# A cached attention block with a gated MLP on one core: the last head's V split by batch, the last w_down chunks in smaller loads, 50 rows of w_down in a load of 25 rows

## The chip, the core and the metric

The kernel runs on one core of a Trainium2 chip. The metric is the device time in microseconds (us), the median of three runs. Beside it stands one execution that the hardware profiler recorded; all durations below come from it, and they count from the start of its span. The core's engines are called as in the profile: PE multiplies matrices (PEld: its weight loads), DVE and ACT work on vectors, POOL is used for sums and maxima across partitions, SP issues the transfers, and 16 DMA engines carry them out.

## What is computed

Two tokens (batch 2, one position each) go through a decode step of two parallel branches, attention over a cache and a bilinear gated MLP, both on the normalised input, and both are added to it. All numbers are 32-bit.

```python
B, D, Hq, Sk, Dh, F = 2, 512, 32, 8192, 128, 1376
def attention(x, k_cache, v_cache, wq, wo):
    W = min(4096, max(256, Sk // 4))                # 2048 last positions
    q = (x @ wq) as (B, 32 heads, 1, 128)
    s = q . k_cache[:, :, Sk - W:, :] * Dh ** -0.5
    o = softmax(s) @ v_cache[:, :, Sk - W:, :]
    return o as (B, 1, 4096) @ wo
def glu(x, w_gate, w_up, w_down):
    return ((x @ w_gate) * (x @ w_up)) @ w_down
xn = layernorm(x)
out = x + attention(xn, ...) + glu(xn, ...)
```

## The kernel before

Nearly all of the work is reading: K and V of 32 heads (2048 positions, 2 batches) and the weights are some 159 MB. They are laid out in one `stream` in the order in which they are used. Each load takes 128 rows (one for each SBUF partition), so a load is named here by its columns of 4 bytes: K or V of a head has CK = 4096 columns (2 batches x 16 positions x 128), `wq` and `wo` 512 a head, a chunk of 128 rows of `w_down` 512 columns.

`blocks` (L45) lists the loads. A unit is K of a head with `wq` of a later one, or V of a head with its `wo`; three units make a load of 13824 columns. The last loads are smaller: K of head 31 with V of head 28 and two chunks of `w_down` (9728 columns), V of 29 with its `wo` (4608), V of 30 with its `wo` (4608), V of 31 (4096), `wo` of 31 with chunks 4 to 6 (2048), chunks 7 and 8 (1024), chunk 9 (512). The 96 rows of `w_down` beyond the ten chunks (FR) are packed in 384 columns, `wr`, in an early load. `pump` (L143) issues the loads in order on SP as buffers come free: three step buffers of up to 13824 columns; V of 29 and 30 share one (`late`), all that follows another (`last`). Two small loads follow the third one on SP: `x_nat`, x in 16 rows, and `carry`, a 9 x 9 matrix with two ones.

`InOrder` (L83) makes PE, DVE, ACT and SP issue their instructions in exactly the order in which the code calls them.

For a head h: `products` (DVE: K times q), `sums` (DVE), `maxima` (DVE, then POOL across partitions), `weights` (ACT: `nm`, the scaled maximum, then one exponential for each batch into `p`, with its sum), `reciprocals`. For its V: `weigh` (L329) does eight matrix products, four row groups of the PSUM bank for each of two batches; `copy_out` (ACT) takes the bank to `o_sb`; `transpose` (L346) picks the diagonal parts with four products and scales them into `oT` (ACT, two instructions a head); `project_o` multiplies by `wo` into `acc`. The profile counts each 32-bit product as two matrix instructions, so eight products are x16. `keep_busy(n)` (L326) is a product of n columns whose result nobody reads.

The two batches stand RB = 8 rows apart in `acc`, so that M = 9 rows are kept of which two are used. Up to head 27 `acc` is [9, 512]; after that it is folded: `accumulate` writes four groups of 128 columns to four groups of 32 partitions (`acc_g`), with `carry` as the matrix that moves the sum so far.

The end (L478 to L531) is written out by hand. In order on PE: V of 26 and 27 with fillers, V of 28, two chunks of `w_down`, the fold, head 28's projection, `values([H-3])` for head 29 with a filler of 512 columns before and one after the transposition, then V of 30, a filler of 512, its transposition, a filler of 256, its projection. V of 31 is done in two halves of the columns: eight products of 256 columns into one bank, eight into another (`o_ps2`, half of the tile `spare_t`, zeroed by DVE just before), ACT copying each half; then its transposition, chunks 4 to 6, its projection, chunks 7 to 9. DVE adds `x_nat` to `acc_g` and SP writes `o_out`.

Of the kernel before, what the change touches and what calls it, by code (L numbers as in the profile page):

```python
# [8 lines left out]
F32 = mybir.dt.float32  # L9
AF = mybir.ActivationFunctionType  # L10
# [6 lines left out]
P = 128  # L17
# [9 lines left out]
LAG = 3  # L27
RB = 8
M = RB * (B - 1) + 1
OUT = P  # L30

CARRY = 72
HG = 4
# [5 lines left out]
STEP = 3 * UNIT  # L39
WD = [(0, 2), (2, 4), (4, 7), (7, NFC - 1), (NFC - 1, NFC)]  # L40
NS = 3
FX = FR // NS


def blocks():  # L45

    def wd(n):
        return [("wd", i, D) for i in range(*WD[n])]

    def k(h):
# [15 lines left out]
    loads += [gu(1) + units[0] + units[1] + wd(0) + [("wr", 0, NS * P)]]  # L73
# [40 lines left out]
def kernel(  # L114
    ctx: ExitStack,
    tc: tile.TileContext,
    x_rows: bass.AP,
    carry_rows: bass.AP,
    stream: bass.AP,
# [86 lines left out]

    oT_ring = [const.tile([P, M], F32, name=f"oT{i}") for i in range(4)]
    for t in oT_ring:
        nc.gpsimd.memset(t, 0.0)

# [117 lines left out]

    def weigh(h, v, parts, first, last):  # L329


        for n, part in enumerate(parts):
            b, i = divmod(part, JG)
            pe.matmul(
                o_ps[bank][32 * i : 32 * i + 8 * B, :], p_t[h][:, b, i, :],
                v[:, FB * n : FB * (n + 1)], start=first and b == 0, stop=last and b == B - 1,
            )
# [8 lines left out]
    def transpose(heads, o_sb):  # L346
# [8 lines left out]
        for h in heads:  # L355
            rec = rec_t.pop(h)
            oT[h] = oT_ring[h % 4]
            for b in range(B):
                c = B * side(h) + b
                act.activation(  # L360
                    oT[h][:, RB * b : RB * b + 1], d[:, c : c + 1], AF.Copy,
                    scale=rec[:, b : b + 1],
                )
# [25 lines left out]

    hT = const.tile([P, 4, NFB, M], F32, name="hT")  # L390
    dve.memset(hT, 0.0)

    hX = const.tile([P, NS, M], F32, name="hX")
    dve.memset(hX, 0.0)
# [15 lines left out]
    def gate():  # L410
# [4 lines left out]
        for i in range(4):  # L415
            t = tr[:, P + i * P // 2 : P + i * P // 2 + NFB * B]
            pe.matmul(t, h_sb[:, i * P : (i + 1) * P], rows, start=True, stop=True)
            act.copy(hT[:, i, :, ::RB], t.rearrange("p (n b) -> p n b", b=B))
        for i in range(NS):
            t = tr[:, P + (2 * i + 1) * P // 4 : P + (2 * i + 1) * P // 4 + NFB * B]  # L420
            f = (NFC % 4) * P + i * FX - FR
            pe.matmul(t, h_sb[:, f : f + P], rows, start=True, stop=True)
            act.copy(hX[FR:, i, ::RB], t[FR:, (NFB - 1) * B :])

    def down(n):
        for c in range(*WD[n]):
# [5 lines left out]
            else:  # L432
                accumulate(hT[:, c % 4, c // 4, :], got["wd", c][0], last=(c == NFC - 1))
            done("wd", c)

    def down_rest():
        wr = got["wr", 0][0]
        pe.matmul(
            acc[:, : NS * P], hT[:FR, NFC % 4, NFC // 4, :], wr[:FR], start=False, stop=False
        )  # L440
        for i in range(NS):
# [92 lines left out]
def laid_out(x):  # L534
# [6 lines left out]
    }  # L541
    carry = np.zeros((M, M), a.dtype)
    first["x"][:] = a.reshape(B, P, NC).transpose(1, 0, 2).reshape(P, B * NC)
    for b in range(B):
# [3 lines left out]
        for n in range(NFB):  # L548
            first["rows"][32 * n + b, n * B + b] = 1.0
        carry[RB * b, RB * b] = 1.0  # L550
    cache = {
# [9 lines left out]
    wd = x["B_w_down"]  # L561
    rest = wd[NFC * P :].reshape(FR, NS + 1, P)

    def field(kind, i):
# [10 lines left out]
        if kind == "wr":  # L575
            last = rest[:, NS, :].reshape(NS, FX, P).swapaxes(0, 1)
            return np.concatenate([rest[:, :NS, :], last]).reshape(P, NS * P)
        if kind == "wd":
# [6 lines left out]
    ]  # L585
    x_rows = np.zeros((D // P, 32 // RB, P), a.dtype)
    x_rows[:, :B] = a.reshape(B, D // P, P).transpose(1, 0, 2)
    return {
        "x_rows": x_rows.reshape(-1, P),
        "carry": carry,  # L590
        "stream": np.concatenate(parts),
# [33 lines left out]
```

## Time and profile before

| what | value |
|---|---|
| device time, median of 3 runs | 377.32 us (377.29 to 377.32) |
| span of the profiled execution, first to last instruction | 375.7 us |
| device time less span | 1.6 us |
| moved by DMA | 159.70 MB, mean 425 GB/s |
| PE busy / DVE busy / ACT busy | 256.5 / 294.6 / 58.7 us |
| mean granted PE clock | 0.795 of full |

The page shows one execution. Busy time says little where stages have different limits: the chain of waits, followed back from the last instruction, and the timeline of the end tell more. In a timeline a line is a group of like instructions of one engine: start, time from the first one's start to the last one's end, engine, line of code, operation, output <- input, sizes, count, and in brackets the idle time before it with what ended it. Nearly all lines say L98, the line in `InOrder` that records every call, so groups are told apart by the names of their tiles. The granted clock of PE is given for windows of time.

### The profile page before, as it was taken

The page shows a single profiled execution, that of the slowest core. Times are in us where ns is not written, and L with a number is a line of the kernel's source. Part 1 is how long each engine was busy: PE and PEld are TensorE (multiplying, and loading weights), DVE is VectorE, ACT ScalarE, POOL GpSimd, SP SyncE. Part 2 cuts the span into 40 slices and gives each one's busy share as a digit, 9 for nine tenths or more (in the row PEclk, how much of TensorE's full clock was granted, in tenths as well). Part 3 has the DMA queues.
Part 4 walks back from the last instruction along what each step waited for, and adds up shares of the span by engine and source line. Part 5 has one row for each costly group of instructions (what it writes and reads, how often), then busy time and mean ns, then how long its engine had stood idle before and what let it go on. Part 6 is the DMA issues. An engine that isn't in the chain of part 4 may idle for free.

```text
span 375.7 us, 2891 instructions
## 1 busy us (share of the span) xinstructions
PE 256.5 (68%) x1100; PEld 88.1 (23%) x1100; DVE 294.6 (78%) x147; ACT 58.7 (16%) x259; POOL 25.3 (7%) x78
## 2 busy tenths in 40 slices
PE   3396696986548487864848676485867639637996
PEld 3241122331112122211222211121212213021334
DVE  3299691998599499769949976994996799599960
ACT  1021001122020211201112020111202011121131
POOL 1001000000000000100000100000000000000010
PEclk9796988899696966859686786976669887556999
DMA  8999999899999999999999999999999999999995
GB/s 327 463 436 454 408 426 471 383 465 432 414 465 394 459 424 424 461 400 453 418 437 449 412 447 424 432 442 430 436 436 424 437 434 436 436 425 424 419 421 226
DMA packets 4382, 159.70 MB, mean 425 GB/s; under 512 B 514, under 2 KB 658, under 8 KB 1042
## 3 DMA queue, kind: packets, MB, share of 16 engines
q1 hardware_dynamic: 4370, 159.54, 98.5%
q8 instruction: 8, 0.13, 0.1%
q14 instruction: 4, 0.03, 0.0%
HBM read 159.47 MB, written 0.07 MB: 425 GB/s over the span
## 4 chain that ended last, share of the span: by engine, by line
DMA 62%; DVE 29%; PE 7%; ACT 1%; issue 0%; SPq 0%; DVEq 0%
DMA step<-in_stream_dram 62%; DVE s L98 14%; DVE step L98 14%; PE o_ps L98 3%; PE q L98 2%; PE acc L98 2%; PE tr L98 1%; DVE m L98 0%; ACT o_sb L98 0%; ACT oT L98 0%; SPq L98 0%; DVE rec L98 0%; DVE o_out L98 0%; DVEq L98 0%
## 5 line engine op out<-in xcount | busy, mean ns | idle before, releaser
L98 DVE TENSOR_TENSOR step<-step,q 128x4096 f32<-128x4096 f32 x31 | 136.6, 4408 | 53.3 <-DMA step<-in_stream_dram 53.3
L98 PE MATMUL q<-step,xnb 128*128 128x512 f32 (+1 forms) x128 | 92.7, 874 | 75.5 <-DMA step<-in_stream_dram 75.5
L98 DVE TENSOR_REDUCE s<-step 128x32 f32<-128x4096 f32 x32 | 141.4, 4419 | 1.1
L98 PE MATMUL o_ps<-step,p 128*16 128x512 f32 (+1 forms) x512 | 69.7, 682 | 10.3 <-DMA step<-in_stream_dram 10.3
L98 PEld LDWEIGHTS q<-step,xnb 128*128 128x128 f32 x128 | 32.2, 275 | 128.9 <-DMA step<-in_stream_dram 79.1
L98 PE MATMUL acc<-step,oT 128*9 128x512 f32 (+1 forms) x88 | 35.2, 554 | 9.3 <-ACT oT L98 8.1
L98 PE MATMUL tr<-first,o_sb 128*128 128x2 f32 (+2 forms) x198 | 27.6, 258 | 15.3 <-ACT o_sb L98 12.8
L98 ACT COPY o_sb<-o_ps 128x512 f32<-128x512 f32 (+1 forms) x24 | 13.8, 576 | 143.1 <-PE o_ps L98 143.1
L98 PEld LDWEIGHTS tr<-first,o_sb 128*128 128x128 f32 x198 | 25.5, 196 | 37.3 <-ACT o_sb L98 32.6
L295 POOL PARTITION_ALL_REDUCE mm<-m x32 | 11.3, 354 | 283.4 <-DVE rec L98 178.9
L98 PEld LDWEIGHTS o_ps<-step,p 128*16 128x16 f32 x512 | 13.5, 106 | 70.4 <-issue 55.2
L98 ACT ACTIVATE nm<-mm 128x2 f32<-128x2 f32 x32 | 6.5, 203 | 129.5 <-POOL mm L295 129.5
L98 ACT ACTIVATE p<-s,nm 128x16 f32<-128x16 f32 x64 | 19.2, 300 | 1.0
L98 ACT ACTIVATE oT<-tr,rec 128x1 f32<-128x1 f32 x64 | 12.2, 260 | 28.3 <-PE tr L98 28.3
L311 POOL PARTITION_ALL_REDUCE sum<-rs x32 | 12.7, 398 | 54.8 <-ACT p L98 54.8
L98 PE MATMUL o_ps<-step,xn 128*2 128x512 f32 (+1 forms) x48 | 12.9, 593 | 0.0
L98 ACT ACTIVATION_READ_ACCUMULATOR p<-s,nm 128x1 f32 x64 | 12.0, 187 | 0.0
L98 DVE TENSOR_TENSOR step<-step,tr 128x4096 f32<-128x4096 f32 x1 | 4.4, 4421 | 9.3 <-DMA step<-in_stream_dram 9.3
L98 PEld LDWEIGHTS acc<-step,oT 128*9 128x9 f32 x88 | 4.3, 91 | 19.5 <-ACT oT L98 13.1
L98 PE MATMUL q<-xnb,mean_w 128*128 128x512 f32 (+1 forms) x18 | 8.5, 563 | 0.0
L98 PE MATMUL acc<-step,hT 128*9 128x128 f32 (+2 forms) x58 | 7.9, 357 | 0.0
L98 DVE TENSOR_REDUCE m<-s 128x2 f32<-128x32 f32 x32 | 5.9, 186 | 1.1
(43 smaller groups left out, 36.5 us busy)
## 6 DMA issues: line engine op xcount, KB each, us to landing
step<-in_stream_dram SPq DMA_DIRECT2D x16, 6912.0 KB, 33.7
step<-in_stream_dram SPq DMA_DIRECT2D x2, 6400.0 KB, 32.6
step<-in_stream_dram SPq DMA_DIRECT2D x1, 6720.0 KB, 45.6
step<-in_stream_dram SPq DMA_DIRECT2D x1, 6656.0 KB, 28.9
step<-in_stream_dram SPq DMA_DIRECT2D x1, 5376.0 KB, 15.4
step<-in_stream_dram SPq DMA_DIRECT2D x1, 4864.0 KB, 30.1
step<-in_stream_dram SPq DMA_DIRECT2D x2, 2304.0 KB, 17.2
step<-in_stream_dram SPq DMA_DIRECT2D x1, 2048.0 KB, 15.9
```

Source lines behind the costliest of these rows:

```text
L98: made = call(*args, **kwargs)
L295: nc.gpsimd.partition_all_reduce(mm, m, P, bass_isa.ReduceOp.max)
L311: nc.gpsimd.partition_all_reduce(sum_t[h], rs, P, bass_isa.ReduceOp.add)
```

## The change

- *V of head 31 by batch.* V of 31 is cut by batch into `vh` 0 and `vh` 1, 2048 columns each. `vh` 0 is appended to the load of V of 29 (4608 becomes 6656 columns); `vh` 1 is a load of its own (2048 in place of 4096). PE does batch 0 (`last_half(0)`, four products of 512 columns) after head 29's projection and ahead of V of 30, and batch 1 after head 30's transposition, where the filler of 256 columns was. Both go to `o_ps2`, which DVE now zeroes ahead of head 30's `products`. ACT copies one half of the columns, DVE the other.
- *The last chunks in smaller loads.* Chunks 8 and 9 are cut into halves of 256 columns (64 of each 128). The loads after `wo` of 31 have 768, 512 and 256 columns in place of 1024 and 512. With the 2048 columns ahead of them these are rows of 8, 3, 2 and 1 KB. The products on the halves have 64 columns (`down_half`).
- *The 96 rows beyond the chunks.* 46 of them go, with x itself, into `wr` (256 columns in place of 384); the other 50 into `wd_tail` by a load of its own, 25 rows of 4 KB, in the place of `x_nat` and `carry`, which go. x is now added by the product with `wr`, whose left side gets ones from `rows`; so the last DVE step is a copy. `gate` has two products and four ACT copies for `wr`, and two of each for `wd_tail`, in place of three and three.
- *M = 2.* The batches stand next to each other; `oT`, `hT`, `hX` shrink, their zeroing goes (but `hX`), and `wd_tail` is zeroed on 32 partitions. Two unused tiles (`pad0`, `pad1`) take up space.

```diff
-RB = 8
-M = RB * (B - 1) + 1
+M = B
-WD = [(0, 2), (2, 4), (4, 7), (7, NFC - 1), (NFC - 1, NFC)]
-NS = 3
-FX = FR // NS
+WD = [(0, 2), (2, 4), (4, 7), (7, 8)]
+HD = D // 2
+HP = P // 2
+NT, FT, FP = 2, 25, 28
+FX = FR - NT * FT
+RX = M + FX
+PADS = 96, 248
...
-    out += [(late, v(H - 3)), (late, v(H - 2)), (last, [("v", H - 1, CK)])]
-    out += [(last, [("wo", H - 1, CO)] + wd(2))]
-    return out + [(last, wd(n)) for n in range(3, len(WD))]
+    out += [(late, v(H - 3) + [("vh", 0, CK // B)]), (late, v(H - 2))]
+    out += [(last, [("vh", 1, CK // B)]), (last, [("wo", H - 1, CO)] + wd(2))]
+    halves = [("wh", (c, n), HD) for c in range(WD[-1][1], NFC) for n in range(2)]
+    out += [(last, wd(3) + halves[:1])]
+    return out + [(last, halves[i : i + 2]) for i in range(1, len(halves), 2)]
...
+    const.tile([P, PADS[0]], F32, name="pad0")
+    wd_tail = const.tile([P, NT * D], F32, name="wd_tail")
+    dve.memset(wd_tail[:32, :], 0.0)
...
-    x_nat = const.tile([P, P], F32, name="x_nat")
-    dve.memset(x_nat, 0.0)
-    sp.dma_start(x_nat[::RB, :], x_rows)
-    carry = const.tile([P, CARRY], F32, name="carry")[:M, :M]
-    sp.dma_start(carry, carry_rows)
+    sp.dma_start(wd_tail[FP : FP + FT, :], tail)
+    carry = rows[:M, :M]
...
+    def down_half(c, n):
+        w = got["wh", (c, n)][0]
+        for g in range(4):
+            pe.matmul(
+                acc_g[32 * g : 32 * g + M, n * HP : (n + 1) * HP], hT[:, c % 4, c // 4, :],
+                w[:, g * HP : (g + 1) * HP], start=False, stop=(c, n) == (NFC - 1, 1),
+            )
+        done("wh", (c, n))
...
     def down_rest():
         wr = got["wr", 0][0]
-        pe.matmul(
-            acc[:, : NS * P], hT[:FR, NFC % 4, NFC // 4, :], wr[:FR], start=False, stop=False
-        )
-        for i in range(NS):
+        for i in range(2):
             pe.matmul(
-                acc[:, NS * P :], hX[FR:, i, :], wr[FR:, i * P : (i + 1) * P],
+                acc[:, HD * i : HD * i + HD], hX[: HP + RX, i, :], wr[: HP + RX],
+                start=False, stop=False,
+            )
+        for i in range(NT):
+            pe.matmul(
+                acc, hX[: FP + FT, 2 + i, :], wd_tail[: FP + FT, i * D : (i + 1) * D],
                 start=False, stop=False,
             )
...
     spare, o_ps2 = spare_t[:, 0, :], spare_t[:, 1, :]
+    dve.memset(o_ps2, 0.0)
     products(h)
...
     reciprocals(h + 1)
-    dve.memset(o_ps2, 0.0)
+    def last_half(b):
+        weigh(H - 1, got["vh", b][0], range(b * JG, (b + 1) * JG), b == 0, b == B - 1, o_ps2)
+        done("vh", b)
+    last_half(0)
     o_sb = pv([H - 2])
     keep_busy(GC)
     transpose([H - 2], o_sb)
-    keep_busy(256)
+    last_half(1)
     project_o(H - 2)
     o_sb = small.tile([P, 4 * DH], F32, name="o_sb", bufs=2)
-    v = got["v", H - 1][0].rearrange("p (n k w) -> p n k w", k=2, w=2 * DH)
-    for k, t in enumerate((o_ps[bank], o_ps2)):
-        for n in range(CK // FB):
-            b, i = divmod(n, JG)
-            pe.matmul(
-                t[32 * i : 32 * i + 8 * B, 0 : 2 * DH], p_t[H - 1][:, b, i, :], v[:, n, k, :],
-                start=(b == 0), stop=(b == B - 1),
-            )
-        act.copy(o_sb[:, 2 * k * DH : 2 * (k + 1) * DH], t[:, 0 : 2 * DH])
-    done("v", H - 1)
+    act.copy(o_sb[:, : 2 * DH], o_ps2[:, : 2 * DH])
+    dve.tensor_copy(o_sb[:, 2 * DH :], o_ps2[:, 2 * DH :])
     bank = 1 - bank
     transpose([H - 1], o_sb)
     down(2)
     project_o(H - 1)
     down(3)
-    down(4)
     o_out = const.tile([P, P], F32, name="o_out")
-    dve.tensor_tensor(o_out, acc_g, x_nat, op=ALU.add)
+    const.tile([P, PADS[1]], F32, name="pad1")
+    for c in range(WD[-1][1], NFC):
+        for n in range(2):
+            down_half(c, n)
+    dve.tensor_copy(o_out, acc_g)
```

More of the change, by code (lines that the diff above doesn't have):

```diff
@@ L116 @@
     tc: tile.TileContext,
-    x_rows: bass.AP,
-    carry_rows: bass.AP,
+    tail: bass.AP,
     stream: bass.AP,
@@ L327, in keep_busy, with weigh @@
         pe.matmul(spare[:, 0:n], mean_w, spare_in[:, 0:n], start=True, stop=True)
-    def weigh(h, v, parts, first, last):
+    def weigh(h, v, parts, first, last, into=None):
+        into = o_ps[bank] if into is None else into
         for n, part in enumerate(parts):
@@ L334, in weigh @@
             pe.matmul(
-                o_ps[bank][32 * i : 32 * i + 8 * B, :], p_t[h][:, b, i, :],
+                into[32 * i : 32 * i + 8 * B, :], p_t[h][:, b, i, :],
                 v[:, FB * n : FB * (n + 1)], start=first and b == 0, stop=last and b == B - 1,
@@ L390 @@
     hT = const.tile([P, 4, NFB, M], F32, name="hT")
-    dve.memset(hT, 0.0)
-    hX = const.tile([P, NS, M], F32, name="hX")
+    hX = const.tile([P, 2 + NT, M], F32, name="hX")
     dve.memset(hX, 0.0)
@@ L417, in gate @@
             pe.matmul(t, h_sb[:, i * P : (i + 1) * P], rows, start=True, stop=True)
-            act.copy(hT[:, i, :, ::RB], t.rearrange("p (n b) -> p n b", b=B))
-        for i in range(NS):
[L420 to L423, printed above, removed]
+            act.copy(hT[:, i, :, :], t.rearrange("p (n b) -> p n b", b=B))
+        f = (NFC % 4) * P
+        own = slice((NFB - 1) * B, NFB * B)
+        for i in range(2):
+            t = tr[HP * i : HP * i + RX, P + P // 4 : P + P // 4 + NFB * B]
+            pe.matmul(t, h_sb[:, f - M : f + FX], rows, start=True, stop=True)
+            act.copy(hX[HP * i : HP * i + RX, i, :], t[:, own])
+            one = rows[HP * i : HP * i + M, 2 * i * B : 2 * i * B + B]
+            act.copy(hX[HP * i : HP * i + M, i, :], one)
+        for i in range(NT):
+            t = tr[: FP + FT, P + (2 * i + 3) * P // 4 : P + (2 * i + 3) * P // 4 + NFB * B]
+            f0 = f + FX + i * FT
+            pe.matmul(t, h_sb[:, f0 - FP : f0 + FT], rows, start=True, stop=True)
+            act.copy(hX[: FP + FT, 2 + i, :], t[:, own])
     def down(n):
@@ L561, in laid_out @@
     wd = x["B_w_down"]
-    rest = wd[NFC * P :].reshape(FR, NS + 1, P)
+    rest = wd[NFC * P :]
+    mixed = np.zeros((2, HP, HD), a.dtype)
+    mixed[:, :RX] = np.concatenate([a, rest[:FX]]).reshape(RX, 2, HD).swapaxes(0, 1)
     def field(kind, i):
@@ L575, in field @@
         if kind == "wr":
-            last = rest[:, NS, :].reshape(NS, FX, P).swapaxes(0, 1)
-            return np.concatenate([rest[:, :NS, :], last]).reshape(P, NS * P)
+            return mixed.reshape(P, HD)
+        if kind == "vh":
+            return cache["v"][H - 1][:, i]
+        if kind == "wh":
+            c, n = i
+            return wd[c * P : (c + 1) * P].reshape(P, 4, 2, HP)[:, :, n].reshape(P, HD)
         if kind == "wd":
@@ L585, in laid_out @@
     ]
-    x_rows = np.zeros((D // P, 32 // RB, P), a.dtype)
-    x_rows[:, :B] = a.reshape(B, D // P, P).transpose(1, 0, 2)
     return {
-        "x_rows": x_rows.reshape(-1, P),
-        "carry": carry,
+        "tail": rest[FX:].reshape(NT, FT, D).swapaxes(0, 1).reshape(FT, NT * D),
         "stream": np.concatenate(parts),
@@ L623 @@
     y = r.results[0]["out_0_dram"]
-    return y[[32 * g + RB * b for b in range(B) for g in range(D // P)]].reshape(B, 1, D)
+    return y[[32 * g + b for b in range(B) for g in range(D // P)]].reshape(B, 1, D)
```

14 lines of the change are left out of this document (5 added, 9 removed).

## The prediction

> **What bounds the kernel now.** I read the page first (share of the span, slices, chain of waits), then the chain in order of time, then the timeline of the last 20 us, then the granted clock by 3.41 us windows.
>
> ```profile
> span 375.7 us, 2891 instructions
> DMA  8999999899999999999999999999999999999995
> q1 hardware_dynamic: 4370, 159.54, 98.5%
> DMA 62%; DVE 29%; PE 7%; ACT 1%; issue 0%; SPq 0%; DVEq 0%
> ```
>
> The transfers are full in every slice: 98.5% of 16 engines' span, from the second microsecond to the end. Nothing in the middle of the kernel can be won or lost but by bytes; the chain calls 29% DVE because DVE's work on K is what frees a buffer for the next load. What the change can move is the tail, so that is where the rest of the reading goes.
>
> ```profile
> 352.22 15.87 DMA step<-in_stream_dram
> 368.13 1.06 PE o_ps L98 x16
> ...
> 373.02 0.29 DVE o_out L98
> ```
>
> After the last big wait (V of head 31, used from 368.13) PE has 4.9 us of work up to 373.02. Was PE or the transfer last? This timeline answers (start, duration, engine, group, and in brackets what ended the idle time before it):
>
> ```profile
> 352.41 0.13 PEld L98 LDWEIGHTS o_ps<-step,p 128*16 128x16 f32 x8 [0.78 <-DMA step<-in_stream_dram]
> 357.86 0.41 PE L98 MATMUL acc<-step,oT 128*9 128x128 f32 x8
> 358.08 1.90 PE L98 MATMUL o_ps<-step,p 128*16 128x512 f32 x16
> 360.88 0.95 PE L98 MATMUL tr<-first,o_sb 128*128 128x2 f32 x8
> 361.69 1.10 PE L98 MATMUL q<-xnb,mean_w 128*128 128x512 f32 x2
> 361.86 0.41 ACT L98 ACTIVATE oT<-tr,rec 128x1 f32<-128x1 f32 x2 [1.23 <-PE tr L98]
> 362.57 0.20 ACT L98 ACTIVATE nm<-mm 128x2 f32<-128x2 f32 x1 [0.30 <-POOL mm L295]
> 363.31 0.19 ACT L98 ACTIVATION_READ_ACCUMULATOR p<-s,nm 128x1 f32 x1
> 363.30 1.91 PE L98 MATMUL o_ps<-step,p 128*16 128x512 f32 x16 [0.17 <-DMA step<-in_stream_dram]
> 365.14 1.12 PE L98 MATMUL q<-xnb,mean_w 128*128 128x512 f32 x2
> 366.92 0.68 PE L98 MATMUL q<-xnb,mean_w 128*128 128x256 f32 x2
> 369.98 1.08 PEld L98 LDWEIGHTS tr<-first,o_sb 128*128 128x128 f32 x8 [0.42 <-ACT o_sb L98]
> 370.12 0.37 ACT L98 COPY o_sb<-q 128x256 f32<-128x256 f32 x1 [0.49 <-PE q L98]
> 371.08 0.84 PE L98 MATMUL acc<-step,hT 128*9 128x128 f32 x24
> 371.74 0.40 PE L98 MATMUL acc<-step,oT 128*9 128x128 f32 x8
> 371.96 0.99 PE L98 MATMUL acc<-step,hT 128*9 128x128 f32 x24
> 372.55 0.12 PEld L98 LDWEIGHTS acc<-step,hT 128*9 128x9 f32 x8 [0.25 <-DMA step<-in_stream_dram]
> ```
>
> The last chunk of w_down made PE wait 0.25 us (372.55), V of head 30 0.17 us (363.30), and V of head 29 not at all: PE was still on head 28's projection (357.86 + 0.41) when its multiplication began at 358.08. So in the tail PE and the stream run level, and PE has some 0.4 us to spare in 15. That is the fact on which the forecast turns: the tail has room for no later start of PE.
>
> **The change, part by part.** Every load has 128 rows, so I count columns of the stream. From the first use of the load that carries V of 28 (352.41) to that of V of 30 (363.30) lie 2 x 4608 columns: 9216 / 10.89 = 846 columns a us. V of 29 landed by that at 352.41 + 4608 / 846 = 357.86.
>
> *Half of V31 rides with V29.* The load of 4608 columns becomes one of 6656, and a load is usable only when all of it is there: 352.41 + 6656 / 846 = 360.28, so 2.42 us later. V of 30 is pushed likewise, to 352.41 + 11264 / 846 = 365.73. The second half of V31 lands where all of it did (13312 columns: 368.15), and the w_down loads end where they ended, since 16896 columns remain 16896. What is won: 0.9 us of PE's work on V31 can be done ahead. What it costs: the stretch from V29 on starts 2.20 us later (360.28 against 358.08), and PE works in program order, so everything of heads 29 to 31 stands behind it.
>
> From there by the old rows. Head 29's oT is done at 361.86 + 0.41 = 362.27, now 364.47. ACT runs in order too: head 31's scaled maximum and exponentials stand behind oT of 29 and took from 362.57 to 363.50, now about 364.51 to 365.44. The new first half of V31 needs these, so it can't start at the end of head 29's projection but at 365.44. Eight multiplications of a head take 363.30 to 365.14 = 1.84 us, so four take 0.9: done at 366.34. V of 30 has been waiting since 365.73; its multiplication starts at 366.34, against 363.30 before: 3.04 us late.
>
> From that start on, old distances: up to the small filler after the transposition 366.92 - 363.30 = 3.62 us. There the filler (0.68 us) gives way to the second half of V31, 0.9, makes 4.5. Then the two copies: ACT's half 0.37 as before, the other half on DVE beside it; DVE's own row for such a copy is the 0.67 us below for 512 columns, so about 0.4 for 256; with hand-overs of about 0.2 that is 5.1. Transposition 369.98 to 371.08 less the 0.1 that it waited for the second copy: 6.1. Down-projection of chunks 4 to 6, 371.08 to 371.74: 6.8. Head 31's projection to 371.96: 7.0. Chunk 7, a third of 0.66: 7.2.
>
> ```profile
> 356.80 0.67 DVE L98 COPY acc_sb<-acc 9x512 f32<-9x512 f32 x1
> 325.11 3.61 PE L98 MATMUL o_ps<-step,p 128*16 128x512 f32 x16 [2.83 <-DMA step<-in_stream_dram]
> ```
>
> Chunks 8 and 9 come in halves: 32 matrix instructions of 64 columns for 16 of 128. No row has 64 columns. If the columns set the price it is the old 0.44 us; if the instruction does, 0.88. The nearest row (0.84 for 24 of 128) doesn't tell them apart, so I take the middle, 0.7: 7.9, and 0.2 until DVE sees the result: 8.1. Output copy at 366.34 + 8.1 = 374.44, against 373.02: **+1.4 us**. The bounds on this part: 64 columns 0.26 less or 0.18 more, the exponentials waited for in part only (0.3 less): +0.9 to +1.7.
>
> *Cover that is gone: the clock.* Between head 28's projection (ends 358.27) and V29 at 360.28 PE now has 2.0 us of nothing, with no filler in it. This is what such a gap did elsewhere in this trace (columns: window, its length, PE busy, PEld, DVE, ACT, POOL, granted clock, DMA share, GB/s):
>
> ```profile
> 54.60:58.01 3.41, 2.16 (x10) 0.77 (x8) 2.72 (x4) 0.17 (x1) 0.36 (x1) 1.00 1.16 503
> 58.01:61.43 3.42, 2.16 (x16) 1.70 (x20) 0.00 (x0) 0.81 (x5) 0.00 (x0) 1.00 1.16 501
> 88.73:92.15 3.42, 2.33 (x9) 0.67 (x8) 3.42 (x1) 0.72 (x4) 0.00 (x0) 1.00 1.17 501
> 92.15:95.56 3.41, 0.00 (x0) 0.00 (x0) 0.30 (x3) 0.89 (x5) 0.75 (x2) 1.00 0.71 308
> 136.52:139.93 3.41, 2.19 (x17) 1.07 (x10) 3.38 (x4) 1.00 (x3) 0.13 (x1) 1.00 1.09 470
> 139.93:143.34 3.41, 3.41 (x5) 1.18 (x4) 3.41 (x1) 0.90 (x5) 0.62 (x2) 0.50 1.16 503
> 317.42:320.84 3.42, 2.20 (x15) 1.25 (x12) 3.42 (x1) 1.30 (x5) 0.00 (x0) 1.00 0.93 404
> 320.84:324.25 3.41, 1.44 (x2) 0.00 (x0) 0.28 (x3) 0.89 (x5) 0.75 (x2) 0.50 1.09 472
> 358.38:361.80 3.42, 3.42 (x27) 1.64 (x20) 3.42 (x1) 0.58 (x1) 0.40 (x1) 1.00 0.99 427
> ```
>
> The clock changes only at edges of such windows. After one with PE busy 2.19 or 2.20 us of 3.41 the next ran at 0.50; after 2.33 it stayed at 1.00, and once (54.60) after 2.16. In the tail of before all windows are full and granted 1.00 (last row). With 2.0 us idle a window keeps 1.4 us of work, well under 2.2; only if the edge cuts the gap nearly in half (each part under 1.2 us, some 0.4 us of the 3.4 us of possible positions) does the clock stay. At 0.50 the multiplication of a head takes 3.61 us in place of 1.90 (325.11 above), so a window of 3.41 us does 1.7 us of work and the chain, which is all PE's there, gets **+1.7 us**. Bounds: 0 (clock kept) and 3.4 (two windows). The fillers make this worse: they run for nothing at half rate in front of the transposition.
>
> [...]
>
> *Bytes and the 25-row load.* 13440 columns become 13312 (-64 KB), x's 8 KB and the carry go, 100 KB come: +28 KB, at the mean 425 GB/s +0.07 us. Bounds: 100 KB in 25 rows of 4 KB need not spread evenly. If five engines carry five rows each, these get 20 KB less 4.5, at 425 / 16 GB/s each +0.6 us, and all others -0.17. Every landing is as late as its slowest engine, so -0.2 to +0.6 on all of the tail; I take +0.1.
>
> [...] No row of this trace shows which engine a row took.
>
> *Edits that cost nothing.*
>
> ```profile
> 325.15 4.42 DVE L98 TENSOR_TENSOR step<-step,q 128x4096 f32<-128x4096 f32 x1 [4.00 <-DMA step<-in_stream_dram]
> 364.37 0.48 DVE L98 MEMSET q<- 128x512 f32 x1
> x_nat<-in_x_rows_dram SPq DMA_DIRECT2D x1, 8.0 KB, 45.3
> ```
>
> The memset of the second bank moves from 364.37 to DVE's wait for head 30's K, 4.00 us idle in this trace; without that cover 0.5. The zeroing for the tail rows is 1024 columns wide, about 0.9 us by the row of 512, at a time when DVE waits for its first load. M = 2 for 9 rows changes the weight loads by nanoseconds. Three more ACT copies in the gate and four projections for four others lie early in the kernel, where a load takes far longer than the work on it. The x addition leaves the last DVE step: a copy for the 0.29 at 373.02, at most 0.02 less.
>
> Sum: 1.4 + 1.7 + 0.1 - 0.0 = +3.2. The profiled execution: span 375.7, so 378.9; what lies outside the span (377.32 - 375.7 = 1.6) stays. **Predicted 380.5 us.**
>
> **The rivals.** *Late, but at full clock*: the gap is cut by an edge, or the clock takes a longer gap to fall. Then +1.5: 378.8. For it: the pair 88.73 / 92.15 with 1.1 us idle and the pair 54.60 / 58.01 with 1.25, that did nothing; against it: 2.0 is longer than both. *The end of the stream decides*: PE makes up its delay, and the last landing sets the end as at 372.55. Then 64 columns after it save 0.1, the output copy 0.02, fewer bytes on the lagging engines 0.2: 377.0, not slower. It needs PE to go from V30 to the end in 372.9 - 365.8 = 7.1 us and to be free at 365.8; the rows give 8.1 and 366.3, so fillers or copies would have to cost 1.5 us less than now. *The small load lands on the engines that are last already*: +0.6 on top of the forecast, 381.1.
>
> **How the numbers follow.** Forecast 0.52, full clock 0.27, stream decides 0.15, small load on top 0.06. I leave out the third case and a little beside: 378.0 to 381.3; the forecast's own range is 379.9 to 381.1. About 0.2% (0.75 us) is what a measurement of this kernel can tell from no change. The third case is mostly within that, seldom beyond: faster 0.05, same 0.11, slower 0.84.
>
> **What would show it.** In the profile of the changed kernel: PE idle about 2 us before head 29's multiplication, ended by a transfer; granted 0.50 in one window after it, else 1.00 (full clock); head 30's multiplication with no wait for its V; no wait of PE for the last w_down halves, and the last DVE step near 376. If PE still waits for the last halves, the third case is right and the forecast's main step wrong. If head 29's V is used before 360, the column count is wrong.

## The result and the profile after

The changed kernel takes 378.50 us (median of 7 runs, 378.15 to 380.38), the kernel before 377.27 us in the same rounds (377.01 to 377.32). The ratio is 1.0046, with a 95% interval of 1.0030 to 1.0062: slower, by half a per cent. (It counts all runs, so it lies above the ratio of the two medians, 1.0033.) The seven runs do not scatter about their median: four lie at 378.15 to 378.50 and three at 379.59 to 380.38. The profiled execution is one of the latter (379.59), so it shows a loss that the median run does not have; both losses are taken apart below.

The page of the changed kernel, the rows that answer to those shown of before (span, DMA share by slices, share of queue 1, chain by engine):

```profile
span 377.8 us, 2886 instructions
DMA  8999999999999999999999999999999999999993
q1 hardware_dynamic: 4494, 159.57, 97.9%
DMA 62%; PE 18%; DVE 17%; ACT 2%; issue 1%; SPq 0%; DVEq 0%
```

The stream is as full as before, except in the last slice, 3 tenths in place of 5: the kernel now runs on longer after its transfers are done. Before, the chain of waits had 7% PE; now it has 18%. The chain in order of time (start, duration, what) shows which part that is:

```profile
342.91 17.00 DMA step<-in_stream_dram
...
359.95 1.91 PE o_ps L102 x16
...
365.00 0.86 PE q L102 x8
365.86 1.72 PE o_ps L102 x16
...
370.47 0.38 ACT o_sb L102
...
371.96 3.11 PE acc L102 x72
...
375.09 0.29 DVE o_out L102
```

The last transfer in this chain is V of 29 with its passenger, in at 359.91. From there to the output copy at 375.09 it is PE without a break, but for one copy by ACT. Before, the last transfer in the chain was V of 31, used from 368.13. The timeline of that stretch follows (start, length, engine, group, and in brackets the idle time before it with what ended it). The profile calls the bank of V of 31, `o_ps2`, by the name of its tile, `q`, and so it calls the fillers' bank.

```profile
358.08 0.40 PE L102 MATMUL acc<-step,oT 128*2 128x128 f32 x8
359.95 1.91 PE L102 MATMUL o_ps<-step,p 128*16 128x512 f32 x16 [1.47 <-DMA step<-in_stream_dram]
364.28 0.31 ACT L102 ACTIVATE p<-s,nm 128x16 f32<-128x16 f32 x1
364.59 0.29 ACT L102 ACTIVATE p<-s,nm 128x16 f32<-128x16 f32 x1
364.82 1.04 PE L102 MATMUL q<-step,p 128*16 128x512 f32 x8
365.40 0.11 PEld L102 LDWEIGHTS o_ps<-step,p 128*16 128x16 f32 x4 [0.46 <-DMA step<-in_stream_dram]
365.68 1.90 PE L102 MATMUL o_ps<-step,p 128*16 128x512 f32 x16
370.47 0.37 ACT L102 COPY o_sb<-q 128x256 f32<-128x256 f32 x1 [0.60 <-PE q L102]
370.87 0.42 DVE L102 COPY o_sb<-q 128x256 f32<-128x256 f32 x1 [5.14 <-ACT o_sb L102]
371.89 1.45 PE L102 MATMUL acc<-step,hT 128*2 128x128 f32 x24
373.52 1.53 PE L102 MATMUL acc<-step,hT 128*2 128x128 f32 x40
```

PE waits 1.47 us for V of 29, and V of 30's product starts at 365.68 in place of 363.30, 2.38 us late. Its first weight load waited for V of 30 too (365.40), but the product itself had no idle time before it: it came right behind the first half of V31 (364.82 and the 0.86 us of the chain). Before the last w_down halves PE waits for nothing any more. And the 24 matrix instructions on chunks 4 to 6, which took 0.84 us before, take 1.45. The windows say why (columns: window, its length, busy PE, PEld, DVE, ACT, POOL, granted clock, DMA share, GB/s):

```profile
358.30:361.71 3.41, 1.94 (x24) 0.37 (x16) 3.41 (x1) 0.00 (x0) 0.34 (x1) 1.00 1.02 438
361.71:365.12 3.41, 3.41 (x28) 1.88 (x28) 0.57 (x3) 1.78 (x8) 0.36 (x1) 1.00 0.94 402
368.54:371.95 3.41, 3.14 (x37) 2.17 (x39) 0.42 (x1) 0.79 (x3) 0.00 (x0) 1.00 0.80 309
371.95:375.36 3.41, 3.10 (x73) 2.37 (x72) 0.27 (x1) 0.41 (x2) 0.00 (x0) 0.50 0.00 0
```

The clock did drop to 0.50, but not behind the gap before V of 29, where it was forecast: that window holds 1.94 us of busy PE, and the next was granted 1.00. It dropped behind a window with 3.14 us of busy PE. Both readings contradict the rule of 2.2 us of busy PE that the prediction took from the profile of before.

### The profile page after: what moved, and what is told of

It is laid out like the page before. It is cut to its first block, busy times and chain, and to the rows that moved or that the text cites. A ratio compares the mean times of both kernels' runs of the same rounds, so it can differ in the third digit from the quotient of the medians.

```text
span 377.8 us, 2886 instructions
## 1 busy us (share of the span) xinstructions
PE 256.1 (68%) x1100; PEld 86.9 (23%) x1100; DVE 295.4 (78%) x147; ACT 58.8 (16%) x261; POOL 25.3 (7%) x74
## 4 chain that ended last, share of the span: by engine, by line
DMA 62%; PE 18%; DVE 17%; ACT 2%; issue 1%; SPq 0%; DVEq 0%
DMA step<-in_stream_dram 62%; DVE step L102 8%; DVE s L102 8%; PE o_ps L102 6%; PE q L102 5%; PE acc L102 5%; PE tr L102 3%; ACT o_sb L102 1%; ACT oT L102 1%; SPq L102 0%; ACT hT L102 0%; DVE o_sb L102 0%; DVE m L102 0%; ACT hX L102 0%; DVE o_out L102 0%
## 5 line engine op out<-in xcount | busy, mean ns | idle before, releaser
L102 PE MATMUL o_ps<-step,p 128*16 128x512 f32 x496 | 68.8, 693 | 13.2 <-DMA step<-in_stream_dram 13.2
L102 PEld LDWEIGHTS q<-step,xnb 128*128 128x128 f32 x128 | 32.1, 273 | 128.0 <-DMA step<-in_stream_dram 77.5
L102 PE MATMUL acc<-step,oT 128*2 128x512 f32 (+1 forms) x88 | 33.9, 548 | 9.1 <-ACT oT L102 9.1
L102 PE MATMUL tr<-first,o_sb 128*128 128x2 f32 (+4 forms) x200 | 26.5, 251 | 15.9 <-ACT o_sb L102 13.1
L102 ACT COPY o_sb<-o_ps 128x512 f32<-128x512 f32 x23 | 13.5, 586 | 146.7 <-PE o_ps L102 146.7
L102 PEld LDWEIGHTS tr<-first,o_sb 128*128 128x128 f32 (+2 forms) x200 | 24.4, 188 | 37.5 <-ACT o_sb L102 32.5
L102 PEld LDWEIGHTS acc<-step,oT 128*2 128x2 f32 x88 | 4.0, 88 | 19.7 <-ACT oT L102 14.6
L102 PE MATMUL acc<-step,hT 128*2 128x128 f32 (+2 forms) x72 | 8.2, 411 | 0.0
L102 DVE RECIPROCAL rec<-sum 128x2 f32<-128x2 f32 x32 | 5.0, 155 | 3.3 <-POOL sum L312 3.3
```

The costliest lines, as they stand in the source:

```text
L102: made = call(*args, **kwargs)
```

## The experiments

Each kernel was compared with runs of the kernel before on the same chip, whose medians lie between 377.29 and 377.35 us.

### One half of the change alone, and the other

First the split of V31 in the kernel before (`v_only`), then all of the change but the split (`rest_only`).

```diff
 # v_only, against the kernel before
-    out += [(late, v(H - 3)), (late, v(H - 2)), (last, [("v", H - 1, CK)])]
+    out += [(late, v(H - 3) + [("vh", 0, CK // B)]), (late, v(H - 2))]
+    out += [(last, [("vh", 1, CK // B)])]
...
 # rest_only, against the changed kernel
-    out += [(late, v(H - 3) + [("vh", 0, CK // B)]), (late, v(H - 2))]
-    out += [(last, [("vh", 1, CK // B)]), (last, [("wo", H - 1, CO)] + wd(2))]
+    out += [(late, v(H - 3)), (late, v(H - 2)), (last, [("v", H - 1, CK)])]
+    out += [(last, [("wo", H - 1, CO)] + wd(2))]
```

> The kernel before with the split of V31 alone (first half with V29, second half after V30, both by batch). Theory A: the whole loss is here, 378.1 to 378.6 us in most runs and up to 380.5 in some, PE idle before head 29's product by 1.5 us or more, no wait of PE for the last w_down load. Rival C: about 377.3, no difference.

Measured: 378.49 us (378.25 to 380.06, 5 runs), ratio 1.0036 (1.0023 to 1.0049). The whole loss is there with the split alone.

> All of the change but the split of V31 (V31 again one load behind V30, cut by columns). Theory A (PE starts heads 29 to 31 late because the first half of V31 is loaded with V29): without it the kernel is not slower than before, and the shorter last products and the 25-row load show: 376.8 to 377.1 us, the last w_down landing about 0.3 us earlier than the 372.5 of before. Rival C (the 25-row load or the small last loads hold the stream up): 378 us or more here too.

Measured: 378.01 us (377.14 to 379.81, 12 runs), ratio 1.0018 (1.0007 to 1.0029): far from theory A, and just inside the range that rival C named. The cause that C gives is not seen, though. C has the stream held up, which would lengthen the span. The spans of these runs are 375.3 to 376.9 us with a median of 375.6, against 375.5 for the kernel before; but device time less span, which is 1.7 to 1.9 us in the runs of all the other kernels here, is 1.77 to 3.03 here. So most of the excess of the median lies outside the span, where no engine's instruction is recorded; three of the twelve spans are also longer, 376.3 to 376.9. What either is stays open. The value of the rest of the change is therefore read from another pair, below.

### The load that V of 29 shares

`half_behind30` is the changed kernel with both halves of V31 loaded behind V of 30. `own_load` leaves the first half where it is, but as a load of its own, so that V of 29 need not wait for it.

```diff
 # half_behind30, against the changed kernel
-    out += [(late, v(H - 3) + [("vh", 0, CK // B)]), (late, v(H - 2))]
+    out += [(late, v(H - 3)), (late, v(H - 2)), (last, [("vh", 0, CK // B)])]
...
-    last_half(0)
     o_sb = pv([H - 2])
     keep_busy(GC)
     transpose([H - 2], o_sb)
-    last_half(1)
+    last_half(0)
     project_o(H - 2)
+    last_half(1)
...
 # own_load, against the changed kernel
-    out += [(late, v(H - 3) + [("vh", 0, CK // B)]), (late, v(H - 2))]
+    out += [(late, v(H - 3)), (late, [("vh", 0, CK // B)]), (late, v(H - 2))]
```

> The changed kernel, with the first half of V31 loaded behind V30 and multiplied after head 30's transposition, the second half after its projection; all else as changed. Theory A: V29 and V30 land where they did before, PE has V31's first half done when the second lands, and the stream decides the end: 376.6 to 376.9 us. Rival B (the split by batch is itself dear: eight products into one bank, copies on two engines): 378 us or more, as in the changed kernel.

Measured: 377.48 us (377.30 to 377.69, 11 runs), ratio 1.0004 (0.9996 to 1.0013). The loss is gone with the place of the load, and so is the scatter; the gain that was expected beside it did not come.

> The changed kernel, but the first half of V31 is a load of its own between V of 29 and V of 30; the products stay where they are. V of 29 then lands when it did before the change (357.9), V of 30 as late as in the changed kernel (365.4). Theory A1 (the wait for V of 29, whose load is larger, makes the loss): the loss goes, 377.4 to 377.7. Theory A2 (V of 30, pushed back by the 2048 columns, is as late by itself): head 29 is done earlier, but V of 30 is used from 365.4 in place of 365.7, and from there it is 8.0 us to the output copy: 373.4, so 378.0 to 378.3.

Measured: 378.27 us (378.12 to 378.62, 6 runs), ratio 1.0027 (1.0016 to 1.0039), as theory A2 had it. The timeline of `own_load`:

```profile
358.54 1.90 PE L102 MATMUL o_ps<-step,p 128*16 128x512 f32 x16
363.74 1.05 PE L102 MATMUL q<-step,p 128*16 128x512 f32 x8 [0.15 <-ACT p L102]
365.71 1.91 PE L102 MATMUL o_ps<-step,p 128*16 128x512 f32 x16 [0.92 <-DMA step<-in_stream_dram]
373.72 0.29 DVE L102 COPY o_out<-acc 128x128 f32<-128x128 f32 x1 [2.38 <-PE acc L102]
```

V of 29 is used at 358.54 without a wait, and nothing is won: PE is done with the first half of V31 early and stands before V of 30, which 2048 columns more in front of it have pushed back. It starts at 365.71, as in the changed kernel (365.68), and from there it is 8.01 us to the output copy. So the larger load with V of 29 is not needed for the loss: 2048 columns ahead of V of 30 make it by themselves. In the changed kernel both causes came out level, PE through the first half at 365.68 and V of 30 in at 365.36, so that taking away the one wins nothing.

### The clock

`two_fillers` gives the changed kernel two products that nobody reads, 512 columns in the gap before V of 29 and 256 before the last copies. `before_no_filler` takes the fillers of heads 29 and 30 out of the kernel before.

```diff
 # two_fillers, against the changed kernel
     project_o(HF)
+    keep_busy(GC)
     weights(h)
...
     project_o(H - 2)
+    pe.matmul(o_ps[bank][:, 0:256], mean_w, spare_in[:, 0:256], start=True, stop=True)
...
 # before_no_filler, against the kernel before
-    values([H - 3], ((GC,), (GC,)))
+    values([H - 3])
...
     o_sb = pv([H - 2])
-    keep_busy(GC)
     transpose([H - 2], o_sb)
-    keep_busy(256)
     project_o(H - 2)
```

> The changed kernel with two more products that nobody reads: 512 columns in the gap before head 29, 256 columns while the last copies run. Theory D (the scatter of the changed kernel, 378.2 in some runs and 379.6 to 380.4 in others, is the granted clock, which falls after a window in which PE streams columns for less than about 0.38 of the time): no window falls below 0.4, every run lies at 378.1 to 378.5, and the clock is 1.00 from 345 us to the end. Rival (the scatter comes from the transfers): the scatter up to 380 stays.

Measured: 378.60 us (378.35 to 378.71, 5 runs), ratio 1.0032 (1.0020 to 1.0044), up to 0.2 us above the range that was named. In its profile the clock is 1.00 from 344.7 us to the end, and no run reaches 379. Five runs alone would be thin: with a step in three runs of seven, five without one come by chance once in some 16 times. With the two 0.50 windows that the next run provokes, they speak for the clock as what lay above 378.7 in the changed kernel. What is left is the late start of V of 30 (here 366.12) and PE's 8.1 us after it.

> The kernel before, without the four fillers of heads 29 and 30 (512, 512, 512 and 256 columns, results that nobody reads). Theory D (a window of 3.41 us in which less than about 0.38 of the time goes into streaming columns is followed by one at 0.50): windows between two products of a head now keep 0.1 to 0.5, so most runs get one drop or two, each 1.4 to 1.7 us where PE is the bound: scattered, 377.2 to 381, median 378 to 379.5. [...] In numbers of this kernel, without a drop: 376.9 to 377.4, in all runs alike.

Measured: 379.68 us (379.41 to 382.13, 6 runs), ratio 1.0075 (1.0056 to 1.0094). Fillers that do no work are worth 2.4 us to the kernel before. Windows of this run, and below them two of a run described in the next part, `two_tiles` (columns as above):

```profile
358.99:362.40 3.41, 2.20 (x24) 1.14 (x20) 2.79 (x3) 1.10 (x4) 0.36 (x2) 1.00 0.99 423
362.40:365.82 3.42, 3.38 (x24) 0.56 (x24) 0.65 (x2) 0.79 (x5) 0.40 (x1) 0.50 0.98 422
365.82:369.23 3.41, 2.19 (x31) 1.44 (x30) 0.00 (x0) 1.00 (x3) 0.00 (x0) 1.00 0.97 402
369.23:372.64 3.41, 3.41 (x32) 1.62 (x24) 0.00 (x0) 0.74 (x2) 0.00 (x0) 0.50 0.54 217
```

```profile
356.31:359.72 3.41, 2.46 (x27) 1.40 (x26) 3.41 (x3) 1.20 (x7) 0.40 (x1) 1.00 0.97 417
359.72:363.13 3.41, 3.07 (x16) 0.49 (x16) 2.64 (x3) 0.00 (x0) 0.36 (x1) 0.50 1.01 432
```

The busy column does not order these cases: 2.20, 2.19 and 2.46 us were followed by 0.50, and so was 3.14 us in the changed kernel, but 1.94 was followed by 1.00. What orders them in these traces is how long columns stream through PE. Busy time counts more than that: in the transposition of the kernel before, eight matrix instructions of 2 columns make 0.95 us of it (360.88). Four matrix instructions of 512 columns, one for each row group and side by side, take 0.43 us at full clock, as the distance between the weight loads of two such sets in the timeline of the changed kernel shows (start, length):

```profile
360.39 0.12 PEld L102 LDWEIGHTS o_ps<-step,p 128*16 128x16 f32 x4 [0.31 <-issue]
360.82 0.12 PEld L102 LDWEIGHTS o_ps<-step,p 128*16 128x16 f32 x4 [0.31 <-issue]
```

The time in which at least one product streams is an estimate, worked out at that price (at a granted clock of 0.50 twice that: 0.85 us between two such sets, 360.89 to 361.74 in `two_tiles`) from the columns and starts of the matrix instructions in the traces. It is 0.35 of the window 368.54 to 371.95 of the changed kernel (next: 0.50), 0.52 of its window 358.30 to 361.71 (next: 1.00), 0.29 and 0.38 of the first and the third window of `before_no_filler` (next: 0.50 both times), and 0.30 of 356.31 to 359.72 in `two_tiles` (next: 0.50). The 14 traces of this study hold 852 windows at 1.00 with a next one. All 307 with a share of 0.35 or less were followed by 0.50, all 499 with 0.42 or more by 1.00, and the 46 between went both ways. Busy time does not part them: a window with 1.55 us of it was followed by 1.00, one with 3.14 by 0.50, and half of the 852 lie between. Theory D had put the edge at 0.38.

The drop came without a long wait: in the window 358.99 to 362.40 of `before_no_filler`, behind which the clock fell from 1.00 to 0.50, the longest wait of PE was 0.71 us.

```profile
360.80 1.05 PE L98 MATMUL tr<-first,o_sb 128*128 128x2 f32 x8 [0.71 <-ACT o_sb L98]
```

### The copies beside each other, and what is left at the end

`two_tiles` is the changed kernel with a tile of its own for the half that DVE copies.

```diff
+    o_sb2 = const.tile([P, 2 * DH], F32, name="o_sb2")
     act.copy(o_sb[:, : 2 * DH], o_ps2[:, : 2 * DH])
-    dve.tensor_copy(o_sb[:, 2 * DH :], o_ps2[:, 2 * DH :])
+    dve.tensor_copy(o_sb2, o_ps2[:, 2 * DH :])
```

> The changed kernel, but DVE's half of head 31's o_sb goes to a tile of its own. In the trace of the changed kernel DVE's copy (0.42 us) began only when ACT's (0.37) was done, though both halves of the columns were there. Theory A (from V of 29 on everything is PE and what PE waits for): the copies run beside each other, the transposition starts 0.3 to 0.4 us earlier and the end comes as much earlier: 377.8 to 378.1 in runs that keep the clock, median about 378.1 against 378.5. Theory B (the end of the stream or the clock sets the end): no change, 378.5. If both copies can't read the bank at once, DVE still starts after ACT.

Measured: 379.84 us (378.11 to 381.26, 6 runs), ratio 1.0058 (1.0036 to 1.0079). Its timeline:

```profile
360.06 3.41 PE L102 MATMUL o_ps<-step,p 128*16 128x512 f32 x16 [1.29 <-DMA step<-in_stream_dram]
372.07 0.37 ACT L102 COPY o_sb<-q 128x256 f32<-128x256 f32 x1 [0.60 <-PE q L102]
372.48 0.42 DVE L102 COPY o_sb<-q 128x256 f32<-128x256 f32 x1 [5.14 <-ACT o_sb L102]
```

DVE's copy still starts 0.04 us after ACT's ends. Its bracket names ACT's copy as what it waited for. In the changed kernel the distance is the same within 0.01 us (370.47 and 0.37 for ACT, 370.87 for DVE), so a target of its own won nothing. With separate targets, what the two still share is `o_ps2`, which they read; whether that is the cause no run here shows. The scatter is the changed kernel's again, and shows its size: 378.11 and 378.25, then 379.79 to 379.91, then 381.26, one step of some 1.7 and one of 1.4 us. In the profile, taken at 379.79, the drop falls on V of 29's product (3.41 us in place of 1.90).

The last five start from `half_behind30` (377.48) or the kernel before, and ask why the new order gains nothing there. `one_load` loads both halves of V31 in one; `old_last_loads` has the last loads of before; `even_rows` gives the small load 32 rows; `short_filler` cuts a filler; `v_behind_only` puts the order of `half_behind30` into the kernel before, without the rest of the change.

```diff
 # one_load, against half_behind30
-    out += [(late, v(H - 3)), (late, v(H - 2)), (last, [("vh", 0, CK // B)])]
-    out += [(last, [("vh", 1, CK // B)]), (last, [("wo", H - 1, CO)] + wd(2))]
+    out += [(late, v(H - 3)), (late, v(H - 2))]
+    out += [(last, [("vh", 0, CK // B), ("vh", 1, CK // B)])]
+    out += [(last, [("wo", H - 1, CO)] + wd(2))]
...
 # old_last_loads, against half_behind30
-    out += [(last, wd(3) + halves[:1])]
-    return out + [(last, halves[i : i + 2]) for i in range(1, len(halves), 2)]
+    return out + [(last, wd(3) + halves[:2]), (last, halves[2:])]
...
 # even_rows, against half_behind30
-NT, FT, FP = 2, 25, 28
+NT, FT, FP = 2, 32, 32
...
 # short_filler, against half_behind30
-    values([H - 3], ((GC,), (GC,)))
+    values([H - 3], ((GC,), (256,)))
```

> As the kernel with both halves of V31 behind V30, but both in one load of 4096 columns, as before the change; the products stay by batch. Theory E (there the last landing sets the end, 372.5 in the trace, PE is free before): the load of its own for batch 0 is worth nothing unless PE comes late, 377.4 to 377.6. Theory A' (PE is still the bound): batch 0 can only start when all has landed, 368.1 in place of 367.1, and the end comes 0.5 to 0.9 later: 378.0 to 378.4.

Measured: 378.08 us (377.78 to 378.96, 11 runs), ratio 1.0020 (1.0011 to 1.0029): theory A'. PE waited 0.97 us for the one load and was late from there. Behind V of 30, the load by batch is worth 0.6 us. But the kernel before has one load too, and is 0.8 us faster than `one_load`: from the first use of V31 to the output copy it needed 4.9 us (368.13 to 373.02), where `one_load` needs 5.4. So what the load by batch wins is about what the products by batch cost. In the kernel before, ACT copied the first half of the columns while PE multiplied the second, and head 30's projection was done by then; here the projection stands between the two batches, and the two copies stand behind both. The price of each was not measured by itself.

```profile
368.62 1.05 PE q L102 x8
369.68 0.22 PE acc L102 x8
369.89 0.90 PE q L102 x8
...
374.03 0.29 DVE o_out L102
```

> As the kernel with both halves of V31 behind V30, but chunks 7 and 8 in one load and chunk 9 in another, 4 and 2 KB a row, as before the change; the products stay halves of 64 columns. Theory E: the end is the last landing and what PE has left to do then, 16 products of 64 columns instead of 8, some 0.2 us more: 377.6 to 377.8. If PE is the bound: no change.

Measured: 377.38 us (377.19 to 377.80, 11 runs), ratio 1.0003 (0.9994 to 1.0011). Rows of 8, 3, 2, 1 KB in place of 8, 4, 2 bring nothing that can be measured. Theory E falls as it was put, though not for PE being the bound alone. The chains of waits of the two kernels end in different ways, first `half_behind30`, then `old_last_loads`:

```profile
354.61 17.55 DMA step<-in_stream_dram
...
372.20 0.67 PE acc L102 x24
...
372.89 0.29 DVE o_out L102
```

```profile
340.55 6.39 PE o_ps L101 x32
...
369.29 0.38 ACT o_sb L101
...
370.78 1.86 PE acc L101 x72
...
372.67 0.29 DVE o_out L101
```

One ends on a transfer, the other on 32.1 us of PE with only ACT's copy in between, and the output copies are 0.22 us apart. PE and the stream run level here, as before the change.

> As the kernel with both halves of V31 behind V30, with the filler after head 29's transposition 256 columns instead of 512, since in its trace oT of 29 was ready 0.4 us before the filler ended. If PE's program order still sets the end there, 0.2 to 0.4 earlier: 377.1 to 377.3. If the last landing does (372.5): no change, 377.4 to 377.6.

Measured: 377.51 us (377.18 to 379.77, 12 runs), ratio 1.0011 (1.0001 to 1.0021). No gain: the 0.4 us taken from PE's program turns into waits for transfers. In its timeline PE waits before V of 30 and before the second half of V31, where `half_behind30` did not:

```profile
363.17 0.13 PEld L102 LDWEIGHTS o_ps<-step,p 128*16 128x16 f32 x8 [0.31 <-DMA step<-in_stream_dram]
368.05 0.13 PEld L102 LDWEIGHTS q<-step,p 128*16 128x16 f32 x8 [0.23 <-DMA step<-in_stream_dram]
```

One run of the twelve is at 379.77 again. A drop of the clock would fit, but it is not shown: that run has no profile, and in the one that was taken (377.40) the clock is 1.00 throughout the tail.

> As the kernel with both halves of V31 behind V30, but the small load of w_down has 32 rows in place of 25 (28 KB more; 14 rows fewer in wr, whose width stays). In the traces 25 rows landed as 5 pieces. Theory E, with the uneven load as its cause: 5 engines carry 20 KB each against 8 KB on all 16, the latest of the 16 lands 0.2 to 0.4 earlier: 377.1 to 377.3. Theory F (what is late at the end is the engine that instruction fetches of 16 KB fell on): no change, 377.4 to 377.6, or 0.1 more for the bytes.

Measured: 377.96 us (377.75 to 378.66, 11 runs), ratio 1.0017 (1.0008 to 1.0025): slower than `half_behind30`, against both theories. The last transfer that PE waited for came 0.43 us later (372.58 against 372.15), and in the chain of waits DVE's step on K that begins at 338.68 in `half_behind30` begins 0.47 us later in its trace (339.15). 28 KB are 0.07 us at the mean 425 GB/s of the kernel before, so in this pair the kernel with 32 rows is later by more than their bytes; why was not found.

> The kernel before, with V31 by batch in two loads, both behind V30, and nothing else of the change: the other half of the kernel with both halves behind V30 (377.48). If the rest of the change (M of 2, x by the product, 25 rows, last loads) is worth nothing: 377.3 to 377.6. If the rest costs or brings something that the order hides: 377.1 or less, 377.8 or more.

Measured: 377.58 us (377.36 to 377.89, 11 runs), ratio 1.0006 (0.9997 to 1.0014), beside 1.0004 (0.9996 to 1.0013) for `half_behind30`, which differs from it by the whole rest of the change. That rest is worth nothing that can be measured. No version beats the kernel before.

## Why the prediction was right, and where it was wrong

Slower was right, and the range held. The point, 380.5, was 2.0 us above the median; it names what three of the seven runs did (379.59, 379.97, 380.38), while the median run followed the rival *late, but at full clock*, 378.8 against 378.5 measured.

- *The tail has no room for a later start of PE.* Right, and it carries the result: 2048 columns ahead of V of 30 and an end that moves by some 1 us, in the changed kernel, `v_only` and `own_load` alike.
- *The count of columns.* Right: V of 29 forecast at 360.28, used from 359.95; V of 30 at 365.73, in by 365.36. The 6656 columns took the 7.9 us that 846 a us gives; the stretch began 0.3 us earlier in this execution. The prediction had named a use before 360 as the sign of a wrong count. By its letter that sign came, by 0.05 us, but the earlier start explains it; the sign was drawn too tight.
- *The first half of V31 is held until 365.44 by head 31's exponentials.* Wrong: it needs those of batch 0 only, the first of the two (364.28 to 364.59), and ran at 364.82, right behind head 29's projection (364.60) with no idle time of PE. So V of 30's product was 2.38 us late and not 3.04. That PE's work on the first half decides its start was right, but by little: V of 30 was in 0.3 us before PE was free, where the prediction had 0.6, and `own_load` shows that its landing alone gives the same start.
- *8.1 us from there to the output copy.* Right: 8.01 in `own_load`, at full clock. Two small errors inside it cancel: the copies came one after the other and not beside each other, and the 64-column products cost near their lower bound. In `two_fillers`, at full clock, chunk 7 and the four halves take 0.92 us from the first start (373.28) to DVE's copy (374.20); less chunk 7 and the hand-over, 0.2 each as in the prediction, that is 0.5 for the 32 matrix instructions on the halves, near 0.44: here the columns set the price, not the instruction.
- The first term, *+1.4*, came as 0.9 to 1.2: that is how far the four runs at 378.15 to 378.50 lie above 377.27. (Its upper bound adds up to +1.6, not +1.7.)
- *The clock, +1.7.* The size was right, and that the clock falls; the rule and the place were not. A drop costs 1.4 us in the profiled execution (3.11 us of PE at the end against 1.69 for the same 72 instructions in `two_fillers`) and 1.5 to 1.7 where it falls on a head's product (3.41 us against 1.90; runs of 379.8 against 378.2 in `two_tiles`). But the rule of 2.2 us of busy PE was read from the wrong column. By the share of streaming, a window of the changed kernel falls below 0.36 only if it starts between 355.4 and 357.2 or near 368.5, some 2 of 3.41 us of possible positions, and these differ from trace to trace. Three of seven runs lie a step higher, with `v_only` and `two_tiles` nine of 18 (only the profiled ones are seen to have a drop), where the prediction took all positions but 0.4 of 3.4 us. That step, the chance and not the price, is what put a drop into the point forecast. With a chance near one half, it was luck on which side the median of seven runs fell; it fell on the side without a drop, 2 us below the forecast. The low stretch by the last copies was not seen at all.
- *+0.1 for bytes, nothing for the other edits.* Right within what can be measured: `v_behind_only` against `half_behind30`. The trace of the changed kernel shows the 25 rows landing in five parts, between 47.61 and 48.13 us, in line with the five times five rows that the bound had supposed; on which engines these fell no run shows. The rival that they fall on the last ones (381.1) had no run as high.
- *What would show it.* PE idle before head 29's product, 1.47 us for the 2 that were named; no wait for the last halves, and no idle time before head 30's multiplication: seen. The clock at 0.50 right behind that gap: in the profiles of `v_only` and `two_tiles`, not in that of the changed kernel. The last DVE step: 375.09, for "near 376".
- *The end of the stream decides* (377.0, chance 0.15) did not come true: the last halves were waited for no longer.

The rows of `two_fillers` that are used here, first of its chain of waits, then of its timeline:

```profile
372.48 1.69 PE acc L102 x72
```

```profile
373.28 0.85 PE L102 MATMUL acc<-step,hT 128*2 128x128 f32 x40
374.20 0.29 DVE L102 COPY o_out<-acc 128x128 f32<-128x128 f32 x1 [2.46 <-PE acc L102]
```

## What to carry to other kernels

Where an engine in program order and the stream run level, moving bytes forward is not free: whatever they are put in front of lands later, and the work on it with all that stands behind (here 2048 columns ahead of V of 30 put its product 2.38 us later and made the median 1.2 us longer), so a transfer should move ahead only of one that has slack. In this case the columns that stream in a window of 3.41 us tell what the clock does next (a share of 0.35 was followed by 0.50, one of 0.52 by 1.00), and the busy time does not (3.14 and 1.94 us in these two). The position of the windows differs from trace to trace and is to be treated as chance: the changed kernel has two times, 378.15 to 378.50 and 379.59 to 380.38, not one. Work that nobody reads can be worth microseconds: 2.4 us in the kernel before.

## What the runs showed of the hardware

- In these traces the clock follows the share, as estimated above, of a 3.41 us window in which columns stream: behind 0.35 or less the next window ran at 0.50 (307 of 307), behind 0.42 or more it stayed at 1.00 (499 of 499), and the 46 between went both ways. From 0.50 it came back behind every window with a share of 0.79 or more (326 of 326) and never behind one of 0.74 or less (283 of 283); the 14 between went both ways. The tail of one execution lost the clock twice: the windows from 362.40 and from 369.23 in `before_no_filler`. The highest runs, 381.26 in `two_tiles` and 382.13 in `before_no_filler`, have no profile.
- ACT and DVE, copying different columns of `o_ps2`, go one after the other, DVE's copy starting 0.03 to 0.04 us after the end of ACT's, with one target tile (370.84 and 370.87 in the changed kernel) or two (372.44 and 372.48 in `two_tiles`).
- In the one pair of traces, with a load of 32 rows of 4 KB in place of 25 the last transfer that PE waited for came 0.43 us later (372.58 against 372.15); the cause is open.
- One kernel, `rest_only`, had up to 1.1 us more outside its span than any other; this stays open.
